# One weight load moved from SyncE's DMA queue to ScalarE's, in a fused attention and MLP kernel on one core

## The chip, the cores and the metric

The kernel runs on one core of one Trainium2 chip. The time is device microseconds (us) for one execution, lower is better; three executions of the kernel before took 219.57, 219.62 and 220.11 us, and their median, 219.62 us, is the time before.

## The reference, cut to what matters

The input x is 2048 rows of 512 features in bf16. It is normalised per row, then goes through an attention branch with a compressive memory (32 heads of 16, four segments of 512 rows) and a dense branch with SiLU, and both are added to x.

```
xn  = layernorm(x)                                   # 2048 x 512
q, k, v = xn @ wq, xn @ wk, xn @ wv                  # 512 x 512 weights each
for s in 4 segments:                                 # 512 rows each
    a_dot = softmax(qs @ ks.T * scale + mask) @ vs 
    a_mem = (phi(qs) @ M) / (phi(qs) @ z + 1e-6)
    o     = g * a_mem + (1 - g) * a_dot
    M, z  = M + phi(ks).T @ vs, z + sum(phi(ks))
out = x + o @ wo + silu(xn @ w1) @ w2                # w1: 512 x 1792, w2: 1792 x 512
```

## The kernel before, in words

The rows are handled as 16 tiles of 128; four tiles make a segment. Everything stays in SBUF. For each row tile VectorE takes the statistics (`bn_stats`, L284, `bn_aggr`, L287), ScalarE and VectorE make the reciprocal root for the first four tiles (L301, L304), and VectorE writes the normalised tile `xn_t` (L313). For the first four tiles TensorE turns `xn_t` by transposes into a PSUM bank `ptr` (L844), and ScalarE (tiles 0 and 1) or VectorE (tiles 2 and 3) copies it to `xnT` (L850), which has the features on the partitions. Later tiles are turned by a DMA transpose that SyncE issues (L856). The products with wv, wk, wq and w1 read `xnT` and the weights (the helper `product`, L334 for the full array and L336 for four column strips of 32). In the profile the product with wv has `wv_sb` as its moving operand and is written `ps<-wv_sb,xnT`; those with wk and wq have the weights as the stationary operand and are written `ps<-xnT,wk_sb` and `ps<-xnT,wq_sb`.

The attention scores of one step go into one tile of four PSUM banks, `psS` (L723), of which there is one; ScalarE takes the exponential of the whole of it in one instruction (L729, 128x2048, to `Pb`), and the next step's scores wait for that. There are 72 such steps. Between them TensorE does the products, the weighing of v (L790), the dense branch and the output products (`psO`).

What each engine does, and in which order, is written out by hand: the string `ORDER` is a list of words, each of which calls one piece of the kernel (`PIECES`), and the instructions of each engine stand in the order in which the words come. The first words are

```
ones0 ones1 zeros xc0 xd0 xc1 xq0 xi0 Nv0 busy44 xd1 xq1 xc2 busy6 xi1 X0.1 xd2 xq2 Nv1 X1.1 Xa0.1
v0.0.0 v0.0.1 v0.0.2 xs3 xi2 Nv2 xq3 xi3 v0.0.3 X2.1 Xa1.1 k0.1.0 tb Nv3 X3.1 Xv2.1 k0.1.1 Xv3.1
vv0.0 odd omask k0.0.0 k0.0.1 k0.0.2 k0.0.3 ka0.0 fp0.0 q0.0.0 kf0.0 q0.0.1 q0.0.2 q0.0.3 ...
S0 ...
```

Here `busy44` and `busy6` are 50 matmuls on a zeroed tile whose result nobody reads (L863); `Xt.1` turns row tile t on TensorE, `Xa` and `Xv` copy it out; `v0.0.p`, `k0.dt.p` and `q0.dt.p` are quarters of one product with wv, wk and wq in segment 0 (a quarter of a v product is one matmul of 512 columns, a quarter of a k or q product two of 256, on the first two row tiles for p = 0 and 1 and on the last two for p = 2 and 3); `tb` loads the exponential's table on ScalarE (L307); `S0` is the first step of scores and its exponential. TensorE meets wv first, then X2, then wk, then X3, the rest of wk and then wq.

Ahead of all of this, L157 to L181 issue the loads. `load_x` (L157) and `load_w` (L168) issue one DMA each from the queue of the engine that is their first argument. The four row tiles of segment 0 (`x_lo`, 128 KB each) alternate: tiles 0 and 2 from SyncE, 1 and 3 from ScalarE. Then SyncE issues, in this order, wv, wk and wq (512 KB each), the next four row tiles (`x_hi`), the two halves of w1 (L176), eight more row tiles and beta. ScalarE's queue has only the two tiles of x; the next thing on ScalarE is the square root's table load with a one-element activation (L188). w2 and wo are loaded from ScalarE's queue much later (words `lw0` and `lw1`).

Of the kernel before, what the change touches and what calls it, by code (L numbers as in the profile page):

```python
# [92 lines left out]
def kernel(  # L93
# [13 lines left out]
    nc = tc.nc  # L107
# [42 lines left out]
    wk_sb = cpool.tile([P, DT, D], BF16, name="wk_sb")  # L150
# [16 lines left out]
    def load_w(eng, w_sb, W, k0, k1):  # L167
        eng.dma_start(out=w_sb[:, k0:k1, :], in_=W.rearrange("(ko ki) n -> ki ko n", ki=P)[:, k0:k1, :])  # L168

    load_w(nc.sync, wv_sb, A_wv, 0, 4)  # L170
    load_w(nc.sync, wk_sb, A_wk, 0, 4)
    load_w(nc.sync, wq_sb, A_wq, 0, 4)
    load_x(nc.sync, 4, 4)
    for half in range(2):
# [767 lines left out]
```

## Time and profile before

| what | value |
|---|---|
| median of three executions | 219.62 us |
| the profiled execution's own time | 219.77 us |
| its span, from the first to the last instruction | 218.0 us |
| time around the span in that execution | 1.77 us |
| busy share of PE, ACT, DVE, POOL | 98%, 84%, 82%, 58% |
| instructions | 9284 |
| moved by DMA | 19.60 MB |

PE is TensorE's matmuls and PEld its weight loads, DVE is VectorE, ACT ScalarE, POOL GpSimd, SP SyncE; SPq and ACTq are the DMA-issuing instructions of those two. Times in a row of the timeline are the start from the span's beginning, then the time from the first start to the last end of the merged instructions, then the instruction and how many; square brackets give the idle time before it and what ended it. In a table of windows, a row begins with the window and its length; the last two columns are the mean busy share of the 16 DMA engines (above 1 where transfers overlap on an engine) and the GB/s that they moved, with GB as 10^9 bytes. KB in the list of DMA issues is 1024 bytes. The granted TensorE clock is written PEclk. The end of a matmul is modelled, so PE's busy share overstates how well it is used.

### The profile page before, as it was taken

The page shows a single profiled execution, that of the slowest core. Times are in us where ns is not written, and L with a number is a line of the kernel's source. Part 1 is how long each engine was busy: PE and PEld are TensorE (multiplying, and loading weights), DVE is VectorE, ACT ScalarE, POOL GpSimd, SP SyncE. Part 2 cuts the span into 40 slices and gives each one's busy share as a digit, 9 for nine tenths or more (in the row PEclk, how much of TensorE's full clock was granted, in tenths as well). Part 3 has the DMA queues.
Part 4 walks back from the last instruction along what each step waited for, and adds up shares of the span by engine and source line. Part 5 has one row for each costly group of instructions (what it writes and reads, how often), then busy time and mean ns, then how long its engine had stood idle before and what let it go on. Part 6 is the DMA issues. An engine that isn't in the chain of part 4 may idle for free.

```text
span 218.0 us, 9284 instructions
## 1 busy us (share of the span) xinstructions
PE 213.7 (98%) x4003; PEld 115.2 (53%) x4003; DVE 179.1 (82%) x370; ACT 184.2 (84%) x173; POOL 126.1 (58%) x203
## 2 busy tenths in 40 slices
PE   7999999999999999999999999999999999999994
PEld 7666656655544544444454444445454444465553
DVE  5899999999799879557979886888878897868753
ACT  3799999999999999999999999999989998942000
POOL 6066767969568974786666436962796374410000
PEclk9999999999999999999999999999999999999999
DMA  5996249232203231452113131340042120412232
GB/s 184 362 373 144 51 120 248 50 77 53 51 5 99 76 73 30 93 91 46 49 52 99 53 98 28 74 75 9 0 127 74 54 75 6 130 44 74 73 98 80
DMA packets 33257, 19.60 MB, mean 90 GB/s; under 512 B 14784, under 2 KB 33216, under 8 KB 33216
## 3 DMA queue, kind: packets, MB, share of 16 engines
q1 hardware_dynamic: 30448, 16.29, 28.4%
q10 hardware_dynamic: 2768, 2.72, 4.0%
q8 instruction: 31, 0.51, 1.0%
q14 instruction: 10, 0.08, 0.1%
HBM read 9.96 MB, written 2.10 MB: 55 GB/s over the span
## 4 chain that ended last, share of the span: by engine, by line
PE 89%; ACT 6%; DVE 2%; DMA 1%; issue 0%
PE ps L334 23%; PE psO L336 17%; PE ps L336 16%; PE psS L723 10%; PE psO L334 10%; PE psV L790 8%; ACT Pb L729 4%; PE psS L336 4%; DMA x_lo<-in_A_x_dram 1%; DVE stats L284 1%; PE psM L450 1%; ACT ex L421 1%; ACT kT L374 0%; PE ptr L844 0%; ACT th L490 0%; DVE xn_t L313 0%
## 5 line engine op out<-in xcount | busy, mean ns | idle before, releaser
L729 ACT ACTIVATE Pb<-psS 128x2048 bf16<-128x2048 f32 x72 | 135.2, 1878 | 4.5 <-PE psS L723 2.1
L743 POOL TENSOR_SCALAR_AFFINE_SELECT Pb<-Pb 128x512 bf16<-128x512 bf16 (+2 forms) x88 | 61.8, 712 | 22.2 <-ACT Pb L729 19.2
L495 DVE SCALAR_TENSOR_TENSOR hT<-th,ps 128x512 bf16<-128x512 bf16 x56 | 38.0, 682 | 11.2 <-ACT th L490 10.7
L743 POOL TENSOR_SCALAR_AFFINE_SELECT lows<-Pb 64x512 bf16<-64x512 bf16 (+1 forms) x40 | 22.9, 574 | 33.2 <-ACT Pb L729 25.0
L336 PE MATMUL psO<-w_sb,hT 128*32 128x512 bf16 (+2 forms) x692 | 41.0, 320 | 0.0
L334 PE MATMUL ps<-xnT,w_sb 128*128 128x512 bf16 (+1 forms) x178 | 36.3, 330 | 0.0
L490 ACT ACTIVATE th<-ps 128x512 bf16<-128x512 f32 x56 | 33.0, 594 | 3.8 <-DVE ri L558 2.9
L336 PEld LDWEIGHTS <-hT 128*32 128x32 bf16 x860 | 21.0, 96 | 14.8 <-issue 3.1
L336 PE MATMUL ps<-xnT,w_sb 128*32 128x512 bf16 (+1 forms) x408 | 24.6, 349 | 0.0
L334 PE MATMUL psO<-w_sb,hT 128*128 128x512 bf16 (+2 forms) x93 | 23.6, 331 | 0.0
L723 PE MATMUL psS<-qT,k 32*128 32x64 bf16 (+3 forms) x512 | 23.0, 233 | 0.1
L334 PEld LDWEIGHTS <-w_sb 128*128 128x128 bf16 x178 | 16.4, 98 | 12.0 <-issue 1.2
L790 PEld LDWEIGHTS <-Vz 128*32 128x32 bf16 x768 | 15.9, 97 | 9.5 <-issue 0.6
L790 PE MATMUL psV<-Pb,Vz 128*32 128x448 bf16 (+7 forms) x512 | 20.9, 286 | 0.0
L723 PEld LDWEIGHTS <-k 32*128 32x128 bf16 x512 | 9.3, 92 | 21.5 <-issue 20.3
L723 PE MATMUL psS<-qT,kT 16*128 16x448 bf16 (+3 forms) x256 | 14.7, 269 | 0.0
L334 PE MATMUL ps<-xnT,wk_sb 128*128 128x512 bf16 (+1 forms) x67 | 14.4, 329 | 0.0
L334 PEld LDWEIGHTS <-hT 128*128 128x128 bf16 x93 | 8.5, 97 | 9.8 <-issue 2.1
L336 PEld LDWEIGHTS <-w_sb 128*32 128x32 bf16 x408 | 9.8, 96 | 6.7 <-issue 1.7
L827 DVE CAST odd<-psV 128x512 bf16<-128x512 f32 x16 | 11.0, 687 | 2.5 <-PE psV L790 2.2
L397 DVE CAST qT<-ps 128x512 bf16<-128x512 f32 x15 | 10.3, 685 | 3.3 <-PE ps L334 1.8
L336 PE MATMUL psO<-wo_sb,oT 128*32 128x512 bf16 x140 | 13.0, 380 | 0.0
(112 smaller groups left out, 329.9 us busy)
## 6 DMA issues: line engine op xcount, KB each, us to landing
spr<-rz SPq DMA_DIRECT2D x56, 64.0 KB
x_res<-in_A_x_dram SPq DMA_DIRECT2D x16, 128.0 KB
out_dram<-o_out SPq DMA_DIRECT2D x15, 128.0 KB
w_sb<-in_B_w_dram SPq DMA_DIRECT2D x2, 896.0 KB
w_sb<-in_B_w_dram ACTq DMA_DIRECT2D x1, 1792.0 KB
x_hi<-in_A_x_dram SPq DMA_DIRECT2D x2, 512.0 KB
wv_sb<-in_A_wv_dram SPq DMA_DIRECT2D x1, 512.0 KB
wk_sb<-in_A_wk_dram SPq DMA_DIRECT2D x1, 512.0 KB
```

Of the source, the lines that this page charges most:

```text
L284: nc.vector.bn_stats(out=stats[t][:], in_=xs(t, t + 1)[:, 0, :])
L334: return [nc.tensor.matmul(out, lhsT=lhsT, rhs=rhs, start=start, stop=stop, skip_group_check=True)]
L336: nc.tensor.matmul(out[c : c + 32], lhsT=lhsT[:, c : c + 32], rhs=rhs, start=start, stop=stop, tile_position=(0, c), skip_group_check=True,)
L397: copy(out=seg_tile(s, "qT")[:, dt, :], in_=sts[s].pop(("q", dt))[:, :])
L421: nc.scalar.activation(out=ex[:], in_=phi_src(s, of, dt), func=AF.Exp)
L490: nc.scalar.activation(out=th[:], in_=sts[s]["h", ft][:, :], func=AF.Tanh, scale=0.5)
L495: nc.vector.scalar_tensor_tensor(out=st["hT"][:, ft, :], in0=st.pop(("th", ft))[:], scalar=1.0, in1=st.pop(("h", ft))[:, :], op0=ALU.add, ...
L723: nc.tensor.matmul(psS[:, g, c : c + q2 - q1], lhsT=keys[rows], rhs=st["qT"][rows, dt, q1:q2], start=True, stop=True, tile_position=(32 * ...
L729: exp = nc.scalar.activation(out=blocks(Pb, b).rearrange("p y g c -> p g y c"), in_=psS[:, :, :].rearrange("p g (y c) -> p g y c", c=BLOCK ...
L743: over[id(Pb)].append(nc.gpsimd.affine_select(out=out, in_=in_, compare_op=ALU.is_ge, fill=0.0, base=base, pattern=[[0, out.shape[1]], [1, ...
L790: nc.tensor.matmul(psV[32 * g : 32 * g + 32, q0 : q0 + nq].rearrange("p (y c) -> p y c", y=weights.shape[2]), lhsT=Vzs[s % 2][:, kt, 4 * d ...
L827: copy(out=odd[:], in_=sts[s].pop(("psV", 1))[:, :])
```

## The change

The load of wk is issued from ScalarE's queue, where it stands behind row tiles 1 and 3, in place of SyncE's, where it stood between wv and wq. The tile, the source, the size and every reader stay as they are.

```diff
     load_w(nc.sync, wv_sb, A_wv, 0, 4)
-    load_w(nc.sync, wk_sb, A_wk, 0, 4)
+    load_w(nc.scalar, wk_sb, A_wk, 0, 4)
     load_w(nc.sync, wq_sb, A_wq, 0, 4)
     load_x(nc.sync, 4, 4)
```

In ScalarE's order, at the start of the program, the load comes between the two loads of x and the first table load (`x_lo` holds the first four row tiles, `wk_sb` the weight; `spare` is the one-element activation):

```order
 L937 UNCONDITIONAL_BRANCH
 L157 DMA x_lo<-in_A_x_dram 128x512 x2
+L168 DMA wk_sb<-in_A_wk_dram 128x4x512
 L188 ACT_TABLE_LOAD
 L188 ACTIVATE spare<-zraw 128x1
```

ScalarE has one row more, ahead of its first compute instruction. In SyncE's order, also at the start (`wv_sb` and `wq_sb` are the other two weights, `x_hi` the next four row tiles):

```order
 L157 DMA x_lo<-in_A_x_dram 128x512 x2
 L168 DMA wv_sb<-in_A_wv_dram 128x4x512
-L168 DMA wk_sb<-in_A_wk_dram 128x4x512
 L168 DMA wq_sb<-in_A_wq_dram 128x4x512
 L157 DMA x_hi<-in_A_x_dram 128x4x512
```

SyncE has one row less, and wq and all that comes after it stand one place earlier. The orders of TensorE, VectorE and GpSimd are the same.

## The prediction

> **What bounds the kernel now.** I read the chain that ended last first, on the page and then in order of time for the opening 15 us, because the change touches nothing later.
>
> ```profile
> PE 89%; ACT 6%; DVE 2%; DMA 1%; issue 0%
> ```
>
> ```profile
> 0.79 2.81 DMA x_lo<-in_A_x_dram
> ...
> 6.86 0.40 PE ptr L844 x4
> 7.26 0.93 PE ps L334 x4
> 8.19 0.38 PE ptr L844 x4
> 8.57 0.35 PE ps L334 x2
> 8.92 0.22 PE ptr L844 x4
> 9.14 1.13 PE ps L334 x10
> ...
> 10.29 0.59 ACT kT L374
> ...
> 12.39 1.88 ACT Pb L729
> ```
>
> The only DMA in the chain is the load of the first row tile (its 2.81 us of a 218.0 us span are the page's 1%). From 6.86 us on it is TensorE's written order without a break: tile 1 turned, four matmuls of v, tile 2 turned, two matmuls of wk, tile 3 turned, ten more of wk, then ScalarE's copies and the first exponential at 12.39. Nothing behind that is tied to a fixed time: the chain has no later DMA, only TensorE and ScalarE handing work to each other. So a delay before 12.39 on this chain should reach the end one for one, and a load that lands earlier than it is needed is worth nothing.
>
> So the question is when wv, wk and wq land and when TensorE wants them. When it wants them now, by the timeline of TensorE and its weight loads:
>
> ```profile
> 7.14 0.11 PEld L334 LDWEIGHTS <-xnT 128*128 128x128 bf16 x2
> ...
> 8.17 0.23 PEld L844 LDWEIGHTS <-xn_t 128*128 128x128 bf16 x4 [0.48 <-DVE xn_t L313]
> 8.52 0.11 PEld L334 LDWEIGHTS <-wk_sb 128*128 128x128 bf16 x2
> 8.69 0.28 PEld L844 LDWEIGHTS <-xn_t 128*128 128x128 bf16 x4
> 8.92 1.05 PEld L334 LDWEIGHTS <-wk_sb 128*128 128x128 bf16 x10
> 10.03 0.82 PEld L334 LDWEIGHTS <-wq_sb 128*128 128x128 bf16 x8
> 7.15 1.04 PE L334 MATMUL ps<-wv_sb,xnT 128*128 128x512 bf16 x4
> ```
>
> wv is wanted at 7.15, wk at 8.52, wq at 10.03: some 1.4 to 1.5 us apart. How fast the loads come, by windows (last columns: busy share of the DMA engines, GB/s):
>
> ```profile
> 0.00:3.00 3.00, 1.89 (x18) 1.90 (x19) 1.40 (x2) 1.28 (x1) 2.19 (x13) 1.00 0.23 78
> 3.00:4.00 1.00, 1.00 (x12) 1.00 (x11) 0.38 (x1) 0.20 (x1) 1.00 (x3) 1.00 0.99 337
> 4.00:5.00 1.00, 1.00 (x12) 1.00 (x11) 0.97 (x3) 0.29 (x1) 0.28 (x2) 1.00 0.86 278
> 5.00:6.00 1.00, 1.00 (x13) 1.00 (x11) 0.96 (x5) 0.26 (x1) 0.00 (x0) 1.00 1.03 330
> 6.00:7.00 1.00, 0.72 (x13) 0.55 (x12) 1.00 (x5) 0.50 (x4) 0.00 (x0) 1.00 1.06 357
> 7.00:8.00 1.00, 1.00 (x8) 0.39 (x6) 0.93 (x4) 0.71 (x4) 0.00 (x0) 1.00 1.07 367
> 8.00:9.00 1.00, 1.00 (x12) 0.65 (x12) 0.96 (x4) 0.98 (x3) 0.00 (x0) 1.00 1.08 363
> 9.00:10.00 1.00, 1.00 (x13) 0.86 (x10) 0.85 (x3) 0.99 (x2) 0.00 (x0) 1.00 1.10 369
> ```
>
> ```profile
> wv_sb<-in_A_wv_dram SPq DMA_DIRECT2D x1, 512.0 KB
> x_lo<-in_A_x_dram ACTq DMA_DIRECT2D x2, 128.0 KB
> 11.50 0.70 DVE L284 BATCH_NORM_STATS2 stats<-x_hi 128x6 f32<-128x512 bf16 x1 [0.24 <-DMA x_hi<-in_A_x_dram]
> ```
>
> Summed from the start, 0.85 MB have moved by 5.0 us, 1.18 by 6.0, 1.54 by 7.0, 1.90 by 8.0, 2.27 by 9.0 and 2.64 by 10.0. The four tiles of x are 0.52 MB (4 times 128 KB), each weight 0.52 MB more. Served in SyncE's order, wv's last byte moves at 1.05 MB (about 5.6 us), wk's at 1.57 MB (7.1), wq's at 2.10 MB (8.5) and x_hi's at 2.62 MB (9.96). Its reader on VectorE waited for x_hi until 11.50, so a load can be used about 1.5 us after the bulk of it has moved; wk was loaded into the array at 8.52, which makes it at most 1.4. With 1.4 to 1.5, wv is usable at 7.0 to 7.1 (TensorE starts it at 7.15), wk at 8.5 (8.52), wq at 9.9 to 10.0 (10.03). All three arrive just in time, in the order in which they are used, and the DMA engines are full meanwhile. That is what the change touches.
>
> **The change, part by part.**
>
> *SyncE issues one load less.*
>
> ```profile
> 1.71 0.43 SPq L168 DMA_DIRECT2D wv_sb<-in_A_wv_dram  x1
> 2.18 0.51 SPq L168 DMA_DIRECT2D wk_sb<-in_A_wk_dram  x1
> 2.73 0.51 SPq L168 DMA_DIRECT2D wq_sb<-in_A_wq_dram  x1
> ```
>
> wq and all behind it (x_hi, w1, the other x tiles, beta) are issued 2.73 - 2.18 = 0.55 us earlier. That saves nothing: wq was issued at 2.73 and its last bytes moved at 8.5, behind 1.57 MB, and those 1.57 MB still go first. Cover: the queue of bytes. Without it 0.55 us would be the most it could save, and wq is on time as it is.
>
> *ScalarE issues one load more.*
>
> ```profile
> 0.78 0.90 ACTq L157 DMA_DIRECT2D x_lo<-in_A_x_dram  x2
> 1.72 1.28 ACT L188 ACT_TABLE_LOAD   x1 [1.72 <-PEq L926]
> 3.01 0.20 ACT L188 ACTIVATE spare<-zraw 128x1 f32<-128x1 bf16 x1
> 4.63 0.29 ACT L301 ACTIVATE rstd_all<-mv_all,eps 128x1 f32<-128x1 f32 x1 [1.42 <-DVE mv_all L287]
> ```
>
> Queued behind the new issue are the table load, the one-element activation and then the first square root, for which VectorE and the whole opening wait. The issue costs about 0.55 us as on SyncE, so the activation ends at 3.8 in place of 3.2; ScalarE then idled 1.42 us until VectorE's variance at 4.63, of which 0.87 is left. Price zero; the issue would have to take over 1.4 us to show.
>
> *wk now shares the DMA engines with wv.* ScalarE issues wk at about 1.7, the same moment at which SyncE issues wv, and both rings then hold 0.52 MB behind 0.26 MB of x. Two rings do not carry more than one: 337 GB/s at share 0.99 in the one window in which both are busy (3 to 4 us), 330 to 369 with SyncE's alone. What remains is who goes first, and no row of before shows two long loads side by side, so I bound it. If the engines finish SyncE's ring first, or go by the order of issue, wv lands as before and the price is 0. If they alternate evenly, both finish together, when 1.57 MB have moved: 7.1 us, usable at about 8.5, which is where wk was. If ScalarE's ring is served first, wv is last and lands at the same 8.5. So the price has its upper end at even sharing already. I take even sharing, with wv usable at 8.4 (a few tens of KB before the very last byte of the two).
>
> The Trainium skill ("DMA: Bandwidth & Descriptors", sections "Queues, rings and completion order" and "Issuing engines are not separate DMA queues") says that each DMA engine takes turns, packet by packet, between the rings that have work, and that issuing from several engines saves sequencer time alone. The trace agrees with the second half (the 337 GB/s); by the first half the sum is the one below, by service in order of issue it would be zero; no run shown here separates the two.
>
> *What a wv at 8.4 costs.* TensorE works in order, so with v all of X2, wk, X3 wait. The four matmuls of v run at a known pace once nothing else holds them:
>
> ```profile
> 17.95 1.03 PE L334 MATMUL ps<-wv_sb,xnT 128*128 128x512 bf16 x4
> 8.61 1.00 DVE L850 COPY xnT<-ptr 128x512 bf16<-128x512 bf16 x2
> ```
>
> Four take 1.03 us, the last of them 0.38 to its end, so one every 0.22 and 0.88 for four. X2 starts at 8.4 + 0.88 = 9.28 where it started at 8.17: 1.11 us later (X2 had waited 0.48 us for `xn_t`, which hides part of the 1.25 us by which v is late). Behind it X2 ends 0.40 later at 9.68, VectorE's two copies (0.50 each) end at about 10.7 where they ended at 9.61, and the second half of the first k product follows them: 1.1 us late. wk has landed by then, tile 3 was normalised long before, and wq is on time, so the small gaps at 8.40 to 8.52 and before 8.69 close; they lie beside the copies and give back no more than 0.1. kT, k, qT, the scores and the exponential at 12.39 follow at 13.5.
>
> *Sum.* 219.77 (profiled execution) + 1.1 = 220.87; that execution was 0.15 over the median, so against the median 219.62 + 1.1 = 220.7. Ends of this term: 0 (219.6), and wv usable at 8.6 (1.57 MB at 7.1 plus 1.5), which gives X2 at 9.48, 1.3 late, 220.9 by the median.
>
> **The rivals.**
>
> *SyncE's ring keeps its lead* (not slower). If wv gets nearly all of the engines until it is done, it is usable before 7.15, and wk, following it, at 8.5 as before. The price is 0: 219.6. A gain isn't in it: wk earlier than 8.52 lets two matmuls go 0.12 us sooner, but X3 at 8.69 waits for the normalised tile anyway. It decides at wv usable by 7.15 for nothing lost; each 0.1 us beyond 7.3 costs 0.1 (the 0.14 between hides in X2's wait). For it: SyncE issues wv at 1.71, and a 0.5 us lead in generating the transfers would be a third of wv. Against it: both rings start with equal loads of x, issued at 0.78 and 0.79, so neither has a lead.
>
> *The delay is given back later.* VectorE waits for x_hi at 11.50 by 0.24 us now and would not when all else is 1.1 late; if such waits fed the chain, part returns. Against it: the chain holds no DMA and 2% of VectorE. To fall under 0.3% (0.66 us, about what a measurement of this kernel can tell from no change) it must return 0.45 us: 220.2 or less.
>
> *TensorE's clock falls in the stall.*
>
> ```profile
> L863 PE MATMUL psS<-zraw x42: 289/314/314, 1.1 to 5.5; 128*128 128x128 bf16 x42
> L844 PE MATMUL ptr<-ident,xn_t x16: 219/219/230, 6.2 to 8.9; 128*128 128x128 bf16 x16
> 1.11 5.25 PE L863 MATMUL psS<-zraw 128*128 128x128 bf16 x50 [1.11 <-DVE zraw L186]
> ```
>
> The matmuls on zeros take 314 ns until after 5.5 us, the transposes of the same size 219 ns from 6.2 on: TensorE starts at a slow pace (5.25/50 = 0.105 us each) and gets quick after about 4.8 us of work (transposes load at 0.23/4 = 0.06). The PEclk column, 1.00 throughout, does not show it. With wv late there are only eight transposes between the last zeros at 6.4 and 8.4. If that puts TensorE back to half pace for another 4.8 us, it loses 2.4 more: 219.6 + 1.1 + 2.4 = 223.1. Against it: two microseconds with some work are less than half of what the warming took. The Trainium skill ("TensorE: Matmul & The Clock Gate", Part 1) puts the fall at an idle window of about 3.4 us whose phase is free; by that the clock holds here.
>
> **How the numbers follow.** Even sharing and the full delay: 0.62, at 220.7, between 220.4 and 221.1 (0.8 to 1.4 late). SyncE's ring first: 0.17, 219.6. Given back later: 0.06, about 220.1. Clock falls: 0.10, 223.1. Something that makes it over 0.3% quicker, for which I see no path (all loads at the head are already just in time, and the 0.12 us gap is the most that an earlier wk frees): 0.05. So slower 0.62 + 0.10 = 0.72, same 0.17 + 0.06 = 0.23, faster 0.05. The range runs from the rival without a price, 219.6, to 221.3, which takes in the upper end of the delay with the spread of the three runs above their median (up to 0.5) in part; it leaves out the fallen clock and the gain, 0.15 in all.
>
> **What would show it.** Right: in the profile of the changed kernel TensorE's weight loads or matmuls on wv start at 8.3 to 8.6 in place of 7.15, with the idle time before put down to wv's load; X2 near 9.3; the first exponential near 13.5; distances between later rows as before; the DMA windows unchanged. ScalarE's first square root stays at 4.63. Wrong: v at 7.15 (the rings don't share evenly), an exponential at 13.5 with an unchanged end (given back), or matmuls of 128 columns at 314 ns behind the stall (clock).

## The result and the profile after

The changed kernel took 223.28 us (median of six runs, 221.23 to 224.88); the kernel before took 220.23 us beside it (six runs, 219.57 to 221.41). The ratio is 1.0122 with a 95% interval of 1.009 to 1.0155: slower, and above the range that was forecast. A ratio here leaves out runs over 1.5% above the fastest of their kernel, and the changed kernel's own spread is that wide, so the single times with their clocks, further down, say more than the ratio.

The chain that ended last, by engine, in the profile after (an execution of 223.13 us, span 221.4):

```profile
PE 93%; DMA 3%; ACT 2%; SPq 0%; issue 0%; DVE 0%
```

The same chain in order of time, for the opening:

```profile
1.70 7.55 DMA wv_sb<-in_A_wv_dram
...
9.29 1.02 PE ps L334 x4
10.31 0.43 PE ptr L844 x4
...
11.59 3.88 PE ps L334 x25
```

The head of the chain is no longer row tile 0 but the load of wv, 7.55 us from its issue to its landing at 9.25. The trace has sixteen landings for each load, as many as there are DMA engines, and TensorE starts 0.04 us after the last of them. Twelve of wv's sixteen had come by 6.52 us; the other four came between 8.34 and 9.25. (In the kernel before all sixteen lay between 5.56 and 6.89.) The timeline after: TensorE around wv, then ScalarE's first and last exponential; and behind it two rows of the timeline before, the ten matmuls of wk and the last exponential:

```profile
9.29 1.02 PE L334 MATMUL ps<-wv_sb,xnT 128*128 128x512 bf16 x4 [2.03 <-DMA wv_sb<-in_A_wv_dram]
10.15 0.59 PE L844 MATMUL ptr<-ident,xn_t 128*128 128x128 bf16 x4
...
11.39 2.34 PE L334 MATMUL ps<-xnT,wk_sb 128*128 128x256 bf16 x10
...
15.86 1.88 ACT L729 ACTIVATE Pb<-psS 128x2048 bf16<-128x2048 f32 x1
...
193.77 1.88 ACT L729 ACTIVATE Pb<-psS 128x2048 bf16<-128x2048 f32 x1
```

```profile
8.98 1.28 PE L334 MATMUL ps<-xnT,wk_sb 128*128 128x256 bf16 x10
...
190.31 1.88 ACT L729 ACTIVATE Pb<-psS 128x2048 bf16<-128x2048 f32 x1
```

TensorE waited 2.03 us for wv and started it at 9.29 where it had started at 7.15. Tile 2's transposes came at 10.15 for 8.17, 1.98 late. The ten matmuls of wk took 2.34 us where they had taken 1.28. The first exponential came at 15.86 for 12.39, 3.47 late, and the last one 193.77 - 190.31 = 3.46 late. So all of the loss arises before the first exponential, and none is given back. It has two parts: 1.98 us for wv, and 3.47 - 1.98 = 1.49 us between tile 2's transposes and the exponential. The windows of TensorE (PE busy, then the granted clock, the DMA share and GB/s) show the second part. They begin where the trace's record of the granted clock changes, 3.41 us apart:

```profile
6.77:10.19 3.42, 1.39 (x12) 1.00 1.04 353
10.19:13.60 3.41, 3.41 (x22) 0.50 1.07 380
13.60:17.01 3.41, 3.41 (x31) 1.00 1.07 364
```

From 10.19 to 13.60 us the granted clock was 0.50. In the profile before the column has 1.00 in all of the opening; its record of the clock begins only at 5.94 us, so it says nothing of the slow matmuls on zeros ahead of that.

ScalarE's side went as the forecast had it:

```profile
1.72 0.46 ACTq L168 DMA_DIRECT2D wk_sb<-in_A_wk_dram  x1
2.21 1.28 ACT L188 ACT_TABLE_LOAD   x1 [2.21 <-issue]
3.50 0.20 ACT L188 ACTIVATE spare<-zraw 128x1 f32<-128x1 bf16 x1
4.63 0.29 ACT L301 ACTIVATE rstd_all<-mv_all,eps 128x1 f32<-128x1 f32 x1 [0.93 <-DVE mv_all L287]
```

The issue took 0.46 us and moved the table load by 0.49; the first square root stayed at 4.63.

### The profile page after: what moved, and what is told of

Read it like the earlier page. It is cut to its first block, busy times and chain, and to the rows that moved or that the text cites. A ratio compares the mean times of both kernels' runs of the same rounds, so it can differ in the third digit from the quotient of the medians.

```text
span 221.4 us, 9284 instructions
## 1 busy us (share of the span) xinstructions
PE 215.4 (97%) x4003; PEld 116.7 (53%) x4003; DVE 179.3 (81%) x370; ACT 184.3 (83%) x173; POOL 126.1 (57%) x203
## 4 chain that ended last, share of the span: by engine, by line
PE 93%; DMA 3%; ACT 2%; SPq 0%; issue 0%; DVE 0%
PE ps L334 27%; PE psO L336 17%; PE ps L336 16%; PE psS L723 11%; PE psO L334 10%; PE psV L790 8%; PE psS L336 4%; DMA wv_sb<-in_A_wv_dram 3%; ACT Pb L729 2%; PE psM L450 1%; PE ptr L844 0%; SPq L157 0%; PE ps L507 0%; ACT th L490 0%; DVE o_half L667 0%
## 5 line engine op out<-in xcount | busy, mean ns | idle before, releaser
L334 PE MATMUL ps<-xnT,wk_sb 128*128 128x512 bf16 (+1 forms) x67 | 15.7, 355 | 0.0
L415 POOL TENSOR_SCALAR pos<-kT 128x512 bf16<-128x512 bf16 x12 | 8.3, 695 | 10.6 <-ACT kT L374 10.2
```

The source lines that it names most:

```text
L334: return [nc.tensor.matmul(out, lhsT=lhsT, rhs=rhs, start=start, stop=stop, skip_group_check=True)]
L415: nc.gpsimd.tensor_scalar(out=pos[:], in0=phi_src(s, of, dt), scalar1=3.0e38, scalar2=0.0, op0=ALU.min, op1=ALU.max)
```

## The experiments

The theory after this profile: wv comes late because wk goes beside it, and the hole that this leaves in TensorE's work makes its clock fall for one stretch of 3.4 us. Rivals: the half clock comes with the execution and not with the hole; two rings cost time of their own; the order of issue decides and not the turns of two rings.

**e1_cover: the hole filled with work that nobody reads.** Against the changed kernel:

```diff
-... X1.1 Xa0.1 v0.0.0 ...
+... X1.1 Xa0.1 busy28 v0.0.0 ...
```

> The changed kernel with 28 more matmuls on the zeroed tile between TensorE's transposes of row tile 1 and its first matmul of v, about 1.6 us of work nobody reads, inside the 2.03 us for which TensorE waited for wv. Theory (wv is late because two rings share the DMA engines, and the lull in TensorE's work then halves its clock for one 3.4 us stretch): wv still starts at 9.0 to 9.4 us, the granted clock is 1.00 in every window and every run, the first exponential starts at 14.2 to 14.5 in place of 15.86, and the time is 221.6 to 222.2 with little spread. Rival 1 (the half clock comes with the run and not with the lull): a window at 0.5 stays, 223 with the same spread from 221 to 225.

TensorE's timeline and ScalarE's first exponential:

```profile
9.86 1.02 PE L334 MATMUL ps<-wv_sb,xnT 128*128 128x512 bf16 x3 [1.25 <-DMA wv_sb<-in_A_wv_dram]
10.72 0.39 PE L844 MATMUL ptr<-ident,xn_t 128*128 128x128 bf16 x4
...
14.80 1.88 ACT L729 ACTIVATE Pb<-psS 128x2048 bf16<-128x2048 f32 x1
```

Here wv was later than in the first profile, 9.86, and still the clock stayed at 1.00: in this profile, where tile 2's transposes took 0.39 us and not 0.59, and in all six runs (222.09 to 223.07, median 222.37 beside 220.29; ratio 1.011, 1.0089 to 1.0131). The first exponential was 2.41 late with wv 2.71 late; nothing was added by the clock. The rival that the half clock comes with the execution falls. The time is above the expected 222.2 at its median: wv was later than assumed, and the seventeenth exponential came another 0.6 us later, which the kernels without these matmuls do not show. ScalarE waited there for the scores, and what held them back stays open.

**e2_one_ring: wk ahead of wv, both on SyncE's queue.** Against the kernel before:

```diff
-    load_w(nc.sync, wv_sb, A_wv, 0, 4)
     load_w(nc.sync, wk_sb, A_wk, 0, 4)
+    load_w(nc.sync, wv_sb, A_wv, 0, 4)
     load_w(nc.sync, wq_sb, A_wq, 0, 4)
```

> The kernel before with SyncE's loads of wv and wk exchanged: one ring, wk first, wv second. Theory (part of wv's lateness is the bytes that go ahead of it, part is that two rings run the 16 engines unevenly): wv is usable where wk was, 8.4 to 8.5 us, TensorE waits 1.2 to 1.4 for it, X2 starts at 9.3 and the first exponential at 13.5 if the clock holds (time 220.8 to 221.4) or 15 if it falls (222.5 to 223). Rival 2 (only the bytes ahead of wv count, the rings do not matter): wv starts at 9.2 to 9.3 as in the changed kernel.

TensorE's start of wv in the timeline, and TensorE's windows, the first with the hole:

```profile
9.70 0.59 PE L334 MATMUL ps<-wv_sb,xnT 128*128 128x512 bf16 x1 [2.52 <-DMA wv_sb<-in_A_wv_dram]
```

```profile
5.74:9.15 3.41, 1.14 (x17) 1.00 0.99 334
9.15:12.57 3.42, 2.65 (x13) 0.50 1.08 372
```

wv started at 9.70 in this profile, later than in the changed kernel, with one ring. The median was 223.08 us (221.17 to 224.62, ratio 1.011, 1.0072 to 1.0148), the same as the changed kernel's 223.28 within either interval. The expected 8.5 did not come in this profile, and the times do not bear out the thought behind it, that second place on one ring costs less than a shared first place on two.

**e11_one_ring_cover: e2 with the same 28 matmuls as e1.**

Against e2_one_ring:

```diff
-... X1.1 Xa0.1 v0.0.0 ...
+... X1.1 Xa0.1 busy28 v0.0.0 ...
```

> The kernel with wk ahead of wv on SyncE's one queue and the 28 matmuls on zeros in TensorE's lull: the clock is taken out of both, so that this against e1_cover is one ring against two. If wv's lateness is only its place behind (or beside) 512 KB of wk, the two agree: 221.5 to 222.6, clock 1.00. If two rings cost time of their own, this one is 0.5 us or more the quicker, 220.8 to 221.6.

TensorE's start of wv and ScalarE's first exponential:

```profile
8.47 1.03 PE L334 MATMUL ps<-wv_sb,xnT 128*128 128x512 bf16 x4
...
13.41 1.88 ACT L729 ACTIVATE Pb<-psS 128x2048 bf16<-128x2048 f32 x1
```

The median was 222.17 us (five runs, 221.68 to 222.23; ratio 1.01, 1.0085 to 1.0114), against e1's ratio of 1.011. With the clock out of both, one ring and two agree to 0.2%. In this profile wv came at 8.47, right when the 28 matmuls ended; the last of its landings was at 8.41, where e2, with the same order of loads, had it at 9.66. So wv in second place on one ring is not always equally late either: by 7.0 us 1.47 MB had moved here and 1.34 MB in e2. The seventeenth step was longer here too, by 1.0 us against e1's 0.6. That leaves some half a microsecond open between one ring and two, as much as the rival asked for. What the times show is that wv's place, behind or beside wk, is what costs most.

**e3_half: 256 KB of wk on each queue.** Against the kernel before:

```diff
-    load_w(nc.sync, wk_sb, A_wk, 0, 4)
+    load_w(nc.sync, wk_sb, A_wk, 0, 2)
+    load_w(nc.scalar, wk_sb, A_wk, 2, 4)
```

> Half of wk (its first 256 rows, 256 KB) stays on SyncE's queue behind wv, the other half goes to ScalarE's. Theory: wv shares the engines with 256 KB in place of 512, so it is usable at 7.9 to 8.3 us, TensorE waits 0.7 to 1.1, and the time is 220.4 to 221.0, with the clock at 1.00 in most runs. Rival 3 (a long transfer on a second ring delays wv whatever its size): wv at 9.2, time as the changed kernel's.

TensorE's start of wv, and its window with the hole:

```profile
9.04 1.02 PE L335 MATMUL ps<-wv_sb,xnT 128*128 128x512 bf16 x3 [1.82 <-DMA wv_sb<-in_A_wv_dram]
```

```profile
6.60:10.02 3.42, 1.54 (x15) 1.00 1.05 356
```

The median was 221.48 us (twelve runs, 219.62 to 224.84; ratio 1.0031, 1.0002 to 1.0061): 1.2 us over its 220.29 of before, where the changed kernel lost 3.05. That is some four tenths of the loss for half of the dose, but spread wider than expected. Seven runs had a mean clock of 0.998 or more (219.62 to 221.49) and five 0.985 to 0.992 (222.52 to 224.84). In this profile wv came at 9.04, nearer to Rival 3's 9.2 than to the expected 8.3, while the times are well under the changed kernel's, so this run does not settle that rival. The clock held, with 1.54 us of work in the window that holds the hole.

**e4_late: wk on ScalarE's queue, issued at 4.67 us.** Against the kernel before:

```diff
-... xq0 xi0 Nv0 ...
+... xq0 lk xi0 Nv0 ...
...
-    load_w(nc.sync, wk_sb, A_wk, 0, 4)
...
+        "lk": lambda: load_w(nc.scalar, wk_sb, A_wk, 0, 4),
```

> wk stays on ScalarE's queue but is issued behind ScalarE's first square root, at about 4.9 us in place of 1.72, when most of wv has moved. Theory: wv starts at 7.15 to 7.3 as before; wk now shares the engines with wq and is usable at 9.3 to 10.0 in place of 8.5, so TensorE waits about 1 us there, X3 and the first exponential are 0.8 to 1.4 late, time 220.5 to 221.4, more if the clock falls. Rival (ScalarE's queue is slow whenever it carries a weight, or wv is late for another reason than wk beside it): wv at 9.2 again, 223.

The issues of SyncE and ScalarE, TensorE's wait, and two windows of TensorE:

```profile
3.27 1.89 SPq L175 DMA_DIRECT2D w_sb<-in_B_w_dram  x2
4.67 0.39 ACTq L168 DMA_DIRECT2D wk_sb<-in_A_wk_dram  x1
...
14.10 0.61 PE L333 MATMUL ps<-xnT,wk_sb 128*128 128x256 bf16 x2 [5.42 <-DMA wk_sb<-in_A_wk_dram]
```

```profile
10.13:13.55 3.42, 0.00 (x0) 1.00 1.07 373
13.55:16.96 3.41, 2.86 (x16) 0.50 1.08 361
```

And the DMA queues (packets, MB, share of 16 engines; q1 is SyncE's, q10 ScalarE's), first from 4.67 to 8.5 us, where q10 moved nothing, then from 9 to 12 us:

```profile
q1 hardware_dynamic: 1288, 1.31, 103.4%
...
q1 hardware_dynamic: 425, 0.73, 66.0%
q10 hardware_dynamic: 398, 0.41, 40.1%
```

wv had its old place back (TensorE did v from 7.42 us), as expected. But wk was usable only at 14.10, 9.4 us after its issue, where 9.3 to 10.0 had been expected; the time was 228.05 us (226.6 to 229.0; ratio 1.0359, 1.0329 to 1.0389) where 220.5 to 221.4 had been. The engines were full meanwhile (373 GB/s). Until 8.5 us SyncE's queue alone moved, with the rest of wv, wq, x_hi and the first packets of w1, all issued before wk. Then wk and w1 (issued from 3.27 on) went side by side, almost packet for packet; w1's packets are 1792 bytes and wk's 1024. The first stretch looked like service in the order of issue, whichever queue, and the next three kernels test that.

**e5_behind, e9_spaced, e10_spaced_again: wk half a microsecond later.** Against the changed kernel, another load goes onto ScalarE's queue ahead of wk: beta's in e5, the fifth row tile in e9 and e10.

e5:

```diff
+    nc.scalar.dma_start(out=beta_r[:], in_=...)
     load_w(nc.scalar, wk_sb, A_wk, 0, 4)
...
-    nc.sync.dma_start(out=beta_r[:], in_=...)
```

e9 and e10:

```diff
+    load_x(nc.scalar, 4, 1)
     load_w(nc.scalar, wk_sb, A_wk, 0, 4)
     load_w(nc.sync, wq_sb, A_wq, 0, 4)
-    load_x(nc.sync, 4, 4)
+    load_x(nc.sync, 5, 3)
```

> wk stays on ScalarE's queue, but the tiny load of beta (0.2 KB) goes onto that queue ahead of it, so that wk is issued some 0.45 us later than in the changed kernel, just behind wv (about 2.15 us against 1.70) and beside wq. Theory A (transfers are served in the order of issue, whichever queue they come from; in the changed kernel wv and wk were issued 0.02 us apart and so went side by side): wv has its place back and starts between 7.15 and 8.3 us, wk and wq now go side by side, wk is usable at 9.5 to 10.5, and the time is 220.3 to 222.0. Theory B (each engine takes turns between the two queues): 0.45 us does not matter, wv starts at 8.5 to 9.8 and the time is 222.3 to 223.5.

> wk stays on ScalarE's queue, but one row tile (128 KB, the fifth, taken out of the load of the next four) goes onto that queue ahead of it, so that wk is issued some 0.5 us later, behind wv and beside wq, with no tiny rows in the way. Theory A (transfers go in the order of issue across both queues): beside wv there are now 128 KB in place of 512, so wv starts at 7.2 to 7.8 us in place of 7.96 to 9.29; wk and wq go side by side, wk starts at 9.8 to 10.8, and the time is 221.0 to 222.5 with the clock held. Theory B (each engine takes turns between the two queues): wv starts at 8.0 to 9.8, wk after it without a wait, and the time is 221 to 224 as for the changed kernel.

> The same kernel as e9_spaced, a second profile, because the slowest engine's lag differs between executions. The same two readings: wv at 7.2 to 7.8 and a wait at wk (Theory A), or wv at 8.0 to 9.8 and none (Theory B).

e5, two windows of the DMA engines (share and GB/s last):

```profile
5.00:6.00 1.00, 1.00 (x18) 0.83 (x15) 0.96 (x5) 0.29 (x1) 0.00 (x0) 1.00 1.10 87
6.00:7.00 1.00, 0.22 (x5) 0.19 (x4) 1.00 (x5) 0.50 (x4) 0.00 (x0) 1.00 0.38 82
```

e9, ScalarE's issues and TensorE's start of wv, and TensorE's window with the hole and the next; then e10's start of wv and its window with the hole:

```profile
1.71 0.46 ACTq L157 DMA_DIRECT2D x_hi<-in_A_x_dram  x1
2.19 0.51 ACTq L168 DMA_DIRECT2D wk_sb<-in_A_wk_dram  x1
...
9.32 1.87 PE L335 MATMUL ps<-wv_sb,xnT 128*128 128x512 bf16 x4 [2.02 <-DMA wv_sb<-in_A_wv_dram]
```

```profile
5.10:8.51 3.41, 1.48 (x23) 1.00 0.96 311
8.51:11.92 3.41, 2.60 (x11) 0.50 1.08 376
```

```profile
9.33 1.86 PE L335 MATMUL ps<-wv_sb,xnT 128*128 128x512 bf16 x4 [2.06 <-DMA wv_sb<-in_A_wv_dram]
```

```profile
5.87:9.28 3.41, 1.07 (x15) 1.00 1.01 332
```

e5 decides nothing: beta's 0.2 KB in rows of two bytes held the engines at 87 and 82 GB/s for two microseconds, and the time was 225.42 us (223.4 to 227.14, ratio 1.0228, 1.0187 to 1.0269). e9 and e10 have no such rows, and wv came at 9.32 and 9.33 with wk used right behind it: the number of Theory B (8.0 to 9.8, no wait at wk), not of Theory A (7.2 to 7.8 and a wait at wk). e9's time was 224.33 us (four runs, 222.62 to 224.55; ratio 1.0185, 1.0155 to 1.0216), a little above either theory's range, e10's one run 223.25. So half a microsecond of later issue does not give wv its place back: once both queues hold a load, the two go side by side. The Trainium skill ("DMA: Bandwidth & Descriptors", section "Queues, rings and completion order") has the engines take turns between the rings; e9 and e10 agree, with 9.3 us. From 9 us on e4 agrees too, with 398 packets against 425. Turns do not explain why wk's first packet in e4 came only at 8.57 us, 3.9 after its issue; that stays open.

**e6_before_again and e7_after_again, e12_after_timed: the same two kernels once more.**

> The kernel before, a second profile. If the slowest of the 16 engines ends a load by a different lag in every execution, this profile has wk or wq arrive after 8.6 or 10.1 us and TensorE waiting there, with a time up to 221; if the lag belongs to the changed kernel's two queues, wk starts at 8.5 and wq at 10.0 again and the time is 219.6 to 219.8.

> The changed kernel, a second profile. Theory: wv starts between 8.4 and 9.9 us, by how far the slowest engine lags; the granted clock is at 0.5 for one window of 3.4 us if TensorE's matmuls fill under some 45% of the window before (1.39 of 3.42 us did in the first profile), and not at all if more.

> The changed kernel once more, for the spread: each run has its mean granted clock beside its time. If one window of 3.4 us at half clock costs 1.7 us, the runs stand in steps: clock 1.000 at 220 to 221.5, 0.992 at 222 to 223.5, 0.985 at 223.7 to 225. If the clock is not what spreads them, times and clocks do not go together.

e6, the kernel before (219.56 us): TensorE's load of wk and the first exponential:

```profile
8.41 0.11 PEld L334 LDWEIGHTS <-wk_sb 128*128 128x128 bf16 x2 [0.16 <-DMA wk_sb<-in_A_wk_dram]
...
12.28 1.88 ACT L729 ACTIVATE Pb<-psS 128x2048 bf16<-128x2048 f32 x1
```

e7, the changed kernel (220.16 us), TensorE's start of wv, its window with the hole and the next:

```profile
7.96 1.02 PE L334 MATMUL ps<-wv_sb,xnT 128*128 128x512 bf16 x3 [0.72 <-ACT rstd_all L301]
```

```profile
4.83:8.24 3.41, 1.90 (x26) 1.00 1.02 345
8.24:11.65 3.41, 3.36 (x33) 1.00 1.08 365
```

The row of wv names a square root that ended at the same moment; the last of wv's landings was at 7.92.

e12, the changed kernel again (a run with mean clock 0.992), TensorE's start of wv, its window with the hole and the next:

```profile
9.97 1.02 PE L334 MATMUL ps<-wv_sb,xnT 128*128 128x512 bf16 x4 [2.79 <-DMA wv_sb<-in_A_wv_dram]
```

```profile
7.56:10.98 3.42, 1.01 (x7) 1.00 1.09 372
10.98:14.39 3.41, 3.41 (x23) 0.50 1.07 375
```

The kernel before repeats itself: 7.00, 8.41 and 9.91 us for the three weights, against 7.15, 8.52 and 10.03. The changed kernel does not: wv started at 9.29, 7.96 and 9.97 us in three profiles, where e7 had expected 8.4 to 9.9. e12's twelve runs have a median of 223.29 us beside 219.82 (219.63 to 220.39, 17 runs) for the kernel before (ratio 1.0072, 1.0043 to 1.0101, by the same rule as above). All 19 runs of the changed kernel, by their mean granted clock:

```
clock           runs   us
0.999 to 1.000     6   219.82 220.16 221.22 221.23 221.64 221.81
0.991 to 0.992    10   222.98 223.13 223.22 223.25 223.32 223.36 223.76 223.80 223.92 223.96
0.985              3   224.41 224.65 224.88
```

The times stand in steps, close to the expected ones: one window of 3.4 us at half clock is 1.7 of some 221 us, which is the 0.008 between the rows (two such windows at 0.985, as in e9's profile). From row to row the medians rise by 2.1 and 1.3 us. Not all of that need be the clock's, since a later wv makes a run longer by itself as well. None of the 34 runs of the kernel before that were taken beside e1 and e12 had a clock under 0.999.

**e8_columns: a version meant to give the weights more room.** SyncE's queue alone, wv whole, then the first 256 columns of wk and of wq, then the rest. Against the kernel before:

```diff
-    load_w(nc.sync, wk_sb, A_wk, 0, 4)
-    load_w(nc.sync, wq_sb, A_wq, 0, 4)
+    load_c(nc.sync, wk_sb, A_wk, 0, D // 2)
+    load_c(nc.sync, wq_sb, A_wq, 0, D // 2)
+    load_c(nc.sync, wk_sb, A_wk, D // 2, D)
+    load_c(nc.sync, wq_sb, A_wq, D // 2, D)
```

> The kernel before with wk and wq loaded by halves of their columns on SyncE's queue: wv, wk's first 256 columns, wq's first 256, then the second halves, which are wanted only from 12.7 us on. If the loads at the head are just in time and the slowest engine's lag makes TensorE wait for them, the first half of wk has 0.7 us of room and that of wq 1.4, and the time is 219.4 to 220.0 with less spread, against 219.5 to 220.9 before; if rows of 512 bytes move more slowly than rows of 1024, the room is lost and the time is 220 to 221.

The first exponential, and VectorE's first statistics on x_hi:

```profile
12.38 1.88 ACT L734 ACTIVATE Pb<-psS 128x2048 bf16<-128x2048 f32 x1
...
12.80 0.69 DVE L289 BATCH_NORM_STATS2 stats<-x_hi 128x6 f32<-128x512 bf16 x1 [1.54 <-DMA x_hi<-in_A_x_dram]
```

The first exponential stood at 12.38, where it was, so nothing was gained at the head; v itself began at 7.43 here, behind ScalarE's copy, and not at 7.15. The rows of half the length took longer as a whole (281, 304 and 317 GB/s in the microseconds from 6, 8 and 9, against 357, 363 and 369), so that x_hi was used at 12.80 in place of 11.50. The third exponential came 1.24 us late, and the time was 220.65 us beside 220.08 (ratio 1.0025, 1.0009 to 1.004). No version here beats the kernel before.

## Why the prediction was wrong

- *What bounds the kernel*: right. wv, wk and wq are used within 0.15 us of the same times in the second profile of before as well, wk after a wait of 0.16 us for its load, and a delay ahead of the first exponential reached the end whole (3.47 us at the first, 3.46 at the last).
- *SyncE issues one load less, ScalarE one more, both at no price*: right; the square root stayed at 4.63 and ScalarE still idled 0.93 us before it.
- *wk shares the engines with wv, taken as even sharing*: right in kind (e9, e10, e4's packets), too small in size, and the first of two steps that failed. The forecast had wv usable at 8.4 us and at most at 8.6, and so tile 2 at 1.1 late; three profiles gave wv at 9.29, 7.96 and 9.97, and the first of them tile 2 at 1.98 late. The lag of 1.4 to 1.5 us from the bytes to their use was read from SyncE's loads in one profile and held to be a constant. It isn't: it is over when the last of the sixteen landings has come, and these can lie 3.6 us apart (5.68 to 9.25). With one ring too, wv in second place was used at 9.70 (e2). In the three profiles of the changed kernel wv was the later the less had moved by 7.0 us: 1.57 MB with wv at 7.96, 1.46 at 9.29, 1.12 at 9.97. Why the engines differ so stays open.
- *From wv to tile 2*: right. 9.29 + 0.88 = 10.17, measured 10.15.
- *The clock*: the second step that failed, put at nothing in the sum. It stood as a rival with a chance of 0.10, at 223.1 us, and it is what 13 of the 19 runs did. That the rival's time is so near the measured 223.28 is luck: its price was too high and the wait for wv too low. "Two microseconds with some work are less than half of what the warming took" was no measure. Windows at full clock with 0.00 to 1.48 us of TensorE work out of 3.41 were followed by one at half clock (0.00 in e4, 1.01 in e12, 1.07 in e10, 1.14 in e2, 1.39 in the changed kernel, 1.48 in e9); windows with 1.54 us and more were not (1.54 in e3, 1.90 in e7, whose records of the clock begin at 6.60 and 4.83 us). The length of one wait does not decide: in e9 the clock fell at 8.51, when TensorE had stood still for 1.2 us, and in e3 it held over a wait of 1.82. The hole took a window below the bound, and e1 and e11 show that filling it holds the clock. The price of 2.4 us was too high, because the clock came back after one window of 3.4 us and not 4.8: 1.49 us in the first profile. The Trainium skill ("TensorE: Matmul & The Clock Gate", Part 1) asks for an idle window of about 3.4 us; the length of the window is right (3.41), but here a window 30 to 43% full was enough (1.01 to 1.48 us).
- *The sum without the fallen clock*: the six runs at 0.999 and above have a median of (221.22 + 221.23) / 2 = 221.2 us, 1.0 over the 220.23 and 1.4 over the 219.82 of before; 1.1 was forecast. That does not save the term for wv. The clock holds in runs whose hole is small, so these six are probably those with an early wv (7.96 in the only one with a profile). In e1, where the clock held however late wv was, the time was 2.1 us over the kernel before, of which the longer seventeenth step can be 0.6.

## What to carry to other kernels

Loads that arrive just in time in the order of their use are in the right queue already: a second queue does not add bandwidth, it takes from the load that is wanted first. A wait of TensorE at the start should be priced twice, once for itself and once for the clock: look at how full each stretch of 3.4 us is with the hole in it, wherever it may begin, and if that falls under half (the bound lay between 43 and 45% here), fill the hole or expect some 1.5 us more. And a time that comes in steps asks for the clock of each run before any other reason.

## What the runs showed of the hardware

- The clock fell after windows at full clock in which TensorE was busy up to 1.48 us of 3.41, and in these profiles stayed after 1.54 and more. A window at half clock needs more to be followed by a full one: e2's came back with 2.65 us of work, e9's stayed at half for a second window with 2.60. The ends of matmuls are modelled, so these bounds are rough.
- A load of 0.2 KB in rows of two bytes, issued among the large ones, took the DMA engines down to 87 and 82 GB/s for two microseconds, in which the kernel before moved 330 and 357 (e5).
- A load issued from ScalarE at 4.67 us, with SyncE's queue full, moved its first packet 3.9 us later, then took turns with SyncE's, 398 packets against 425 from 9 to 12 us, and was usable 9.4 us after its issue (e4).
- A load was used 0.04 us after the last of its sixteen landings, and in the changed kernel twelve of wv's had come 2.7 us before the last (6.52 and 9.25).
